# Program order for four operations of each float64 weight piece on ScalarE and VectorE

## The chip, the cores and the metric

The kernel runs on one core of a Trainium2 chip. The metric is the device time of one execution in microseconds (us). A core has five instruction streams: TensorE (PE in the profile, with its weight loads as PEld), VectorE (DVE), ScalarE (ACT), GpSimd (POOL) and SyncE (SP), which here only issues transfers. In the trace each engine takes its instructions in the order in which they stand in its stream; one that waits holds up those behind it.

## The reference

```python
X = np.fft.rfft(x, axis=1)                       # x: 8 x 3072 x 256, float32
Xr, Xi = (X.real.astype(np.float32), X.imag.astype(np.float32))
Yr = Xr @ w_r - Xi @ w_i + b_r                   # w_r, w_i: 256 x 256
Yi = Xr @ w_i + Xi @ w_r + b_i
Yr = np.sign(Yr) * np.maximum(np.abs(Yr) - lam, 0.0)      # lam = 0.01; Yi likewise
y = np.fft.irfft(Y, n=x.shape[1], axis=1).astype(np.float32)
...
h = x @ w_in                                     # 24576 rows; w_in 256 x 2048, w_out 2048 x 256: float64
g = np.where(h > 0.0, h, alpha * (np.exp(np.minimum(h, 0.0)) - 1.0))
x = (g @ w_out).astype(np.float32)
...
expert_idx = np.argmax(x @ w_gate, axis=1)       # 8 experts, each takes the first 768 rows that choose it
h = np.maximum(np.einsum('ecd,edf->ecf', disp, w1), 0.0)  # w1: 8 x 256 x 1024, w2: 8 x 1024 x 256
y = np.einsum('ecf,efd->ecd', h, w2)
out[i] = gate_w[i] * y[expert_idx[i], pos[i]]    # rows over the capacity stay zero
```

The inputs w_in and w_out of the middle layer are float64; the kernel has to turn them into float32 pairs itself.

## The kernel before

The kernel has three stages that overlap. In the first, three of the eight batches go through a Fourier transform, a mixing matrix and the transform back; as soon as some of it is there, the middle layer (`Moe.up`, `Moe.down`) begins on tiles of 512 rows; at the end the eight experts run. By then every expert has its 768 rows, so the other batches are never computed.

The first stage is cut into units. One batch has 12 units of work, numbered u0 to u35 over the three batches. The steps, with the lines that the profile shows:

- `s1` (L143 on PE, copies `zo` L145 on ACT, stores to `zs`): the first transform step, 8 pieces in a batch, from tiles `xp` that SP loads.
- `s2` of a unit (L173 on PE): needs the tile `zi`, which SP loads two units ahead into one of three buffers, and for the first 12 units a constant tile `ag`. Its result is split on ACT (`xr` L185, `im` L186, `xs` L199), DVE (`sm` L197, `xr` L198) and POOL (L200).
- `mix` of a unit (L218, L223, L229 on PE; in the plan 2.2 units after its `s2`), then `k` L220 on ACT, `tt` L233 on DVE, `kb` L235 on ACT, `tc` L236 on DVE.
- `i1` (L248 on PE), once for two units, reads their `tc`; ACT copies the result to two tiles `vo` (L252) and stores them to `vs`.
- `i2` (L272 on PE), 16 pieces in a batch, reads tiles `vi` that SP loads from `vs`; ACT copies it into the one buffer `yt` (L273), and every second time stores that to `ys`, from which the middle layer loads its rows `y`.

PSUM banks are shared: `s1`, `i1` and `i2` take turns on three banks (`pd`), `mix` on three others. So a late `zo`, `vo` or `yt` copy on ACT holds up the third PE step behind it.

Into this stage the float64 weights are worked, in 16 pieces of 128 x 512 values, called p0 to p15 here (8 of w_in, 8 of w_out). `f64_parts` handles one piece in four steps, which the plan puts at 0, 1.35, 1.5 and 1.85 units from the piece's time; pieces follow each other every 27/16 units. SP loads the raw words into the tile `fv` (512 KB); ACT squares the high words (L388); DVE selects (L390), shifts the low words out of `fv` (L392), and builds the float32 value (L393, L394); ACT rounds it to the first part (L396); DVE (L397, L399) and POOL (L398, L400) make the second part. The pool of these tiles has one buffer, so `fv` of a piece can be loaded only after L392 of the piece before, its last reader.

What order do the engines see? The Python code is traced in the plan's order. A scheduler then sorts each engine's stream: an instruction whose inputs it takes as ready goes ahead of one that would still wait, and of two ready ones the one that was traced first goes first. All loads on SP are exempt, since `load` wraps them:

```python
def load(tc, dst, src, eng=None):
    tc.keep_in_program_order((eng or tc.nc.sync).dma_start(dst, src))
```

`keep_in_program_order` ties an instruction behind the one that was traced just before it on the same engine. It adds no wait; it only fixes the place in the stream.

Of the kernel before, what the change touches and what calls it, by code (L numbers as in the profile page):

```python
# [14 lines left out]
AF = mybir.ActivationFunctionType  # L15
ALU = mybir.AluOpType
# [94 lines left out]
def load(tc, dst, src, eng=None):  # L111

    tc.keep_in_program_order((eng or tc.nc.sync).dma_start(dst, src))


def f32(ap):
    return ap.bitcast(F32)
# [256 lines left out]
def f64_parts(tc, tmp, src, p1, p2):  # L374

    nc, n = tc.nc, int(np.prod(src.shape[1:]))
    v = tmp.tile([128, 2 * n], I32, name="fv").rearrange("p (n t) -> p n t", t=2)
    sv = src.bitcast(I32)
    load(tc, v, sv.rearrange("p (n t) -> p n t", t=2) if len(sv.shape) == 2
                      else sv.rearrange("p a (n t) -> p a n t", t=2))  # L380
    yield
    hi, lo = v[:, :, 1], v[:, :, 0]
    sq = tmp.tile([128, n], F32, name="fsq")
    h = tmp.tile([128, n], I32, name="fh")
    a = tmp.tile([128, n], I32, name="fa")
    b = tmp.tile([128, n], I32, name="fb")
    least = float(np.array([0x380C0000], np.uint32).view(np.float32)[0])
    nc.scalar.activation(sq, f32(hi), AF.Square)  # L388
    yield
    nc.vector.scalar_tensor_tensor(f32(h), sq, least * least, f32(hi), op0=ALU.is_ge, op1=ALU.mult)  # L390
    low = sq.bitcast(I32)
    nc.vector.tensor_scalar(low, lo, 1, None, op0=ALU.logical_shift_right)  # L392
    nc.vector.tensor_scalar(a, h, 3, 0x3FFFFFF8, op0=ALU.logical_shift_left, op1=ALU.bitwise_and)  # L393
    nc.vector.scalar_tensor_tensor(b, h, -0x40000000, a, op0=ALU.bitwise_and, op1=ALU.bitwise_or)  # L394
    yield
    nc.scalar.copy(p1, f32(b))  # L396
    nc.vector.tensor_scalar(a, b, -0x00800000, None, op0=ALU.bitwise_and)  # L397
    nc.gpsimd.tensor_tensor(f32(b), f32(b), f32(p1), op=ALU.subtract)  # L398
    nc.vector.scalar_tensor_tensor(f32(h), low, 2.0 ** -51, f32(a), op0=ALU.mult, op1=ALU.mult)  # L399
    nc.gpsimd.tensor_tensor(p2, f32(b), f32(h), op=ALU.add)  # L400


# [9 lines left out]
def f64_piece(tc, tmp, w_in, w_out, win, wout, i):  # L412

    if i < 8:
        a, c = divmod(i, 4)
        sl = slice(c * 512, c * 512 + 512)
        return f64_parts(tc, tmp, w_in[a * 128:a * 128 + 128, sl], *(w[:, a, sl] for w in win))
    else:
        fs = slice(2 * (i - 8), 2 * (i - 8) + 2)
        return f64_parts(tc, tmp, w_out.rearrange("(f p) d -> p f d", p=128)[:, fs, :],  # L420
                  *(w[i - 8].rearrange("p f d -> p (f d)") for w in wout))
# [683 lines left out]
```

## Time and profile before

| what | value |
|---|---|
| median of 3 runs | 1209.8 us (1209.31 to 1209.97) |
| the profiled execution | 1211.05 us, of which its span (first to last instruction) is 1209.1 us |
| PE busy | 1164.1 us (96%) |
| DVE, ACT, POOL busy | 783.3 (65%), 721.6 (60%), 305.3 (25%) |
| mean granted TensorE clock | 0.985 of full speed |

The profiled execution lies 1.25 us above the median of the runs, and 1.95 us of it lie outside the span. PE is nearly always busy, so the time can only move where PE waits, or where its clock is lowered.

### The profile page before, as it was taken

Reading aid. Unit: us, or ns where it says so; the run is one execution under the profiler, and the core shown is the slowest. Engines: PE = TensorE matmul, PEld = TensorE weight load, DVE = VectorE, ACT = ScalarE, POOL = GpSimd, SP = SyncE. Lnnn points to the kernel's source line nnn. Section 1 sums busy time; section 2 is a strip of 40 time slices with the busy share of each in tenths; the row PEclk is TensorE's granted clock in tenths of the full one; section 3 lists DMA queues with packets and bytes.
Section 4 is the critical chain, followed back from the end, with each engine's and each line's share of the span. In section 5 each row is a group of like instructions: output and inputs, shape, how many; then the busy total and the mean of one; then the engine's idle time right before and its main releaser. Section 6 shows DMA issues by size and latency. Waiting matters only on the chain.

```text
span 1209.1 us, 21128 instructions
## 1 busy us (share of the span) xinstructions
PE 1164.1 (96%) x7800; PEld 1058.9 (88%) x7800; DVE 783.3 (65%) x2022; ACT 721.6 (60%) x1397; POOL 305.3 (25%) x347
## 2 busy tenths in 40 slices
PE   7799998999999999999999999999999999999994
PEld 2577797889999999999999999999999999999994
DVE  1588557553778777687777987887888544444430
ACT  4467676666776766656667666666665444444431
POOL 1244333310112222123122322222154211111111
PEclk9899898999999999999999999999999999999997
DMA  9888785644211211334225232222221323233300
GB/s 268 284 267 240 216 242 170 221 144 156 77 50 45 72 36 53 94 105 141 86 74 162 88 106 88 88 84 78 77 90 44 126 101 118 98 108 103 104 23 24
DMA packets 122912, 143.65 MB, mean 119 GB/s; under 512 B 9090, under 2 KB 106227, under 8 KB 122672
## 3 DMA queue, kind: packets, MB, share of 16 engines
q1 hardware_dynamic: 69360, 70.41, 19.5%
q10 hardware_dynamic: 48496, 59.17, 14.5%
q0 software_dynamic: 4944, 12.64, 3.0%
q8 instruction: 63, 1.03, 0.4%
q14 instruction: 49, 0.40, 0.1%
HBM read 71.96 MB, written 71.15 MB: 118 GB/s over the span
## 4 chain that ended last, share of the span: by engine, by line
PE 61%; issue 20%; DMA 6%; POOL 5%; DVE 4%; ACT 2%; POOLq 0%; SPq 0%; ACTq 0%; DVEq 0%
PE pm L486 25%; PE pa L463 24%; POOL out L405 4%; PE fi L272 3%; PE fmix L229 2%; PE fs L143 2%; PE fi L248 2%; PE fs L173 1%; DMA fv<-in_moe_w_in 1%; PE fmix L218 1%; DMA ys<-yt 1%; DMA zs<-zo 1%; DVE lw L515 1%; POOL g L471 1%; DMA xp<-in_x 1%
## 5 line engine op out<-in xcount | busy, mean ns | idle before, releaser
L486 PEld LDWEIGHTS pm<-wout,g 128*128 128x128 f32 x2640 | 346.1, 191 | 18.1 <-POOL g L471 1.3
L486 PE MATMUL pm<-wout,g 128*128 128x256 f32 x2640 | 352.7, 283 | 0.7 <-POOL g L471 0.5
L463 PE MATMUL pa<-x,win 128*128 128x512 f32 (+1 forms) x1344 | 345.4, 392 | 0.2 <-DVE e L469 0.2
L463 PEld LDWEIGHTS pa<-x,win 128*128 128x128 f32 x1344 | 236.9, 189 | 37.6 <-DVE e L469 0.7
L515 DVE SCALAR_TENSOR_TENSOR lw<-row,wg 128x256 bf16<-128x256 f32 x432 | 220.5, 510 | 7.0
L470 ACT CAST g<-e 128x512 fp32r<-128x512 f32 (+1 forms) x224 | 136.8, 612 | 127.9 <-DVE e L469 124.6
L469 DVE SCALAR_TENSOR_TENSOR e<-pa,e 128x512 f32<-128x512 f32 (+1 forms) x224 | 151.0, 678 | 77.5 <-ACT e L468 77.2
L467 ACT ACTIVATE e<-pa 128x512 f32<-128x512 f32 (+1 forms) x224 | 132.0, 590 | 70.0 <-PE pa L463 63.1
L471 DVE TENSOR_TENSOR g<-e,g 128x512 fp32r<-128x512 f32 x170 | 123.3, 727 | 66.3 <-ACT g L470 63.4
L668 DVE SCALAR_TENSOR_TENSOR eh<-eup,eh 128x384 fp32r<-128x384 f32 x128 | 71.1, 557 | 137.6 <-ACT eh L667 137.5
L666 PE MATMUL eup<-ex,ew 128*128 128x384 f32 x768 | 149.4, 340 | 0.3 <-DVE eh L668 0.3
L678 PE MATMUL edown<-ew,eh 128*128 128x256 f32 x1152 | 142.9, 280 | 0.0
L468 ACT ACTIVATE e<-e 128x512 f32<-128x512 f32 (+1 forms) x224 | 139.2, 625 | 5.2 <-ACT e L467 0.6
L678 PEld LDWEIGHTS edown<-ew,eh 128*128 128x128 f32 x1152 | 139.3, 188 | 0.0
L471 POOL TENSOR_TENSOR g<-e,g 128x512 fp32r<-128x512 f32 (+1 forms) x54 | 66.7, 1239 | 274.5 <-ACT g L470 207.6
L666 PEld LDWEIGHTS eup<-ex,ew 128*128 128x128 f32 x768 | 130.8, 188 | 0.8 <-DVE eh L668 0.6
L405 POOL DMA_INDIRECT out<-eo,er x48 | 46.7, 973 | 213.2 <-ACT eo L681 212.9
L667 ACT ACTIVATE eh<-eup 128x384 fp32r<-128x384 f32 x128 | 62.9, 492 | 60.4 <-PE eup L666 60.2
L681 ACT ACTIVATE eo<-edown,er 128x256 f32<-128x256 f32 x48 | 22.8, 475 | 89.8 <-PE edown L678 46.2
L405 POOL DMA_INDIRECT tab<-row,sl x55 | 57.2, 1040 | 51.7 <-DVE sl L570 38.6
L143 PE MATMUL fs<-xp,f 96*96 96x512 f32 x96 | 50.8, 665 | 10.0 <-DMA xp<-in_x 5.4
L272 PE MATMUL fi<-f,vi 96*128 96x96 f32 (+1 forms) x384 | 49.4, 272 | 3.1 <-DMA vi<-vs 2.6
(125 smaller groups left out, 1211.1 us busy)
## 6 DMA issues: line engine op xcount, KB each, us to landing
out<-row ACTq DMA_DIRECT2D x48, 512.0 KB, 3.5
ewraw<-in_moe_w SPq DMA_DIRECT2D x29, 512.0 KB, 3.6
xp<-in_x SPq DMA_DIRECT2D x24, 384.0 KB, 5.6
zs<-zo ACTq DMA_DIRECT2D x24, 384.0 KB, 5.0
zi<-zs SPq DMA_DIRECT2D x36, 256.0 KB, 5.1
vs<-vo ACTq DMA_DIRECT2D x36, 256.0 KB, 2.8
vi<-vs SPq DMA_DIRECT2D x48, 192.0 KB, 2.7
y<-ys SPq DMA_DIRECT2D x26, 256.0 KB, 3.6
```

Of the source, the lines that this page charges most:

```text
L272: nc.tensor.matmul(pv[:, j, :], v[:, j, :], self.k["f2"][:, 0:m])
L405: i = tc.nc.gpsimd.indirect_dma_start(dst, bass.IndirectOffsetOnAxis(idx, 0), src, None, bounds_check=rows - 1, oob_is_err=False)
L463: nc.tensor.matmul(ps, l, r, start=n == 0, stop=n == len(ops) - 1)
L467: nc.scalar.activation(e, ps, AF.Exp)
L468: nc.scalar.activation(e, e, AF.Relu, bias=1.0, scale=-1.0)
L469: nc.vector.scalar_tensor_tensor(e, ps, 0.0, e, op0=ALU.max, op1=ALU.subtract)
L470: nc.scalar.copy(g1, e)
L471: (nc.gpsimd if (f % 4 == 3 or self.tiles[c] < 4) and f < NF - 1 else nc.vector).tensor_tensor(g2, e, f32(g1), op=ALU.subtract)
L486: nc.tensor.matmul(self.pm[c][h][:, o, :], l[:, ts], r[f // 2][:, f % 2, :], start=f == 0 and o == 0 and n == 0, stop=f == NF - 1 and (o = ...
L515: self.tc.keep_in_program_order(v.scalar_tensor_tensor(T("lw", [128, D], BF16), row[:, t, 0:D], 1.0, rt["wg"][:, e, :], op0=ALU.mult, op1= ...
L666: nc.tensor.matmul(ps, l, r, start=i == 0, stop=i == len(ops) - 1)
L678: nc.tensor.matmul(ps, l[:, f, ts], r[:, f, :], start=f == 0 and i == 0, stop=f == NFE - 1 and i == 2)
```

## The change

Four of the operations of each piece are wrapped in `keep_in_program_order`: both on ACT, and on DVE the two that read what ACT or another step made. The instructions, their operands, buffers and loads stay the same. One line is added to the file, so that the line numbers from 388 on are one higher in the changed kernel (L389 is its square, L391 its select, L393 its shift).

```diff
     least = float(np.array([0x380C0000], np.uint32).view(np.float32)[0])
-    nc.scalar.activation(sq, f32(hi), AF.Square)
+    inorder = tc.keep_in_program_order
+    inorder(nc.scalar.activation(sq, f32(hi), AF.Square))
     yield
-    nc.vector.scalar_tensor_tensor(f32(h), sq, least * least, f32(hi), op0=ALU.is_ge, op1=ALU.mult)
+    inorder(nc.vector.scalar_tensor_tensor(f32(h), sq, least * least, f32(hi), op0=ALU.is_ge, op1=ALU.mult))
     low = sq.bitcast(I32)
     nc.vector.tensor_scalar(low, lo, 1, None, op0=ALU.logical_shift_right)
     nc.vector.tensor_scalar(a, h, 3, 0x3FFFFFF8, op0=ALU.logical_shift_left, op1=ALU.bitwise_and)
     nc.vector.scalar_tensor_tensor(b, h, -0x40000000, a, op0=ALU.bitwise_and, op1=ALU.bitwise_or)
     yield
-    nc.scalar.copy(p1, f32(b))
+    inorder(nc.scalar.copy(p1, f32(b)))
     nc.vector.tensor_scalar(a, b, -0x00800000, None, op0=ALU.bitwise_and)
     nc.gpsimd.tensor_tensor(f32(b), f32(b), f32(p1), op=ALU.subtract)
-    nc.vector.scalar_tensor_tensor(f32(h), low, 2.0 ** -51, f32(a), op0=ALU.mult, op1=ALU.mult)
+    inorder(nc.vector.scalar_tensor_tensor(f32(h), low, 2.0 ** -51, f32(a), op0=ALU.mult, op1=ALU.mult))
     nc.gpsimd.tensor_tensor(p2, f32(b), f32(h), op=ALU.add)
```

How the streams of the engines change: SP's stays as it was, row by row. On ACT and DVE the operations of every piece move to a later place among the others (by 3 to 19 rows on ACT, by 0 to 11 on DVE), up to the end of p15. PE's stream changes only in the first and the second batch, up to the mix of u17, and the same instructions stand in it.

DVE at the first piece (p0), before. `fs_391`, `fs_473` and `fs_523` are the `s2` results of u2, u3 and u4; `k_415` and `k_497` belong to the mix of u0 and u1:

```order
L198 TENSOR_TENSOR xr_364<-fs_358,xr_363 128x512
L192 MEMSET xe 128x4
L390 SCALAR_TENSOR_TENSOR fh<-fsq,fv 128x512
L392 TENSOR_SCALAR fsq<-fv 128x512
L393 TENSOR_SCALAR fa<-fh 128x512
L394 SCALAR_TENSOR_TENSOR fb<-fh,fa 128x512
L197 TENSOR_TENSOR sm<-fs_391,im 128x256
L198 TENSOR_TENSOR xr_397<-fs_391,xr_396 128x512
```

The same place in DVE's stream in the changed kernel:

```order
L197 TENSOR_TENSOR sm<-fs_391,im 128x256
L198 TENSOR_TENSOR xr_397<-fs_391,xr_396 128x512
L197 TENSOR_TENSOR sm<-fs_473,im 128x256
L233 TENSOR_TENSOR tt<-fmix,k_415 128x512
L198 TENSOR_TENSOR xr_479<-fs_473,xr_478 128x512
L236 SCALAR_TENSOR_TENSOR tc<-tt,kb 128x512
L391 SCALAR_TENSOR_TENSOR fh<-fsq,fv 128x512
L233 TENSOR_TENSOR tt<-fmix,k_497 128x512
L393 TENSOR_SCALAR fsq<-fv 128x512
L394 TENSOR_SCALAR fa<-fh 128x512
```

The shift that frees `fv` (L392, now L393) has moved behind the `tc` of u0 and the `tt` of u1.

ACT at the fourth piece (p3), as a piece of the difference. `fi_758` is the first half of the second `i1`, `fs_741` the `s2` of u7:

```order
 L199 CAST xs_691<-sm 128x256
-L185 CAST xr_746<-fs_741 128x512
 L186 COPY im<-fs_741 128x256
-L388 ACTIVATE fsq<-fv 128x512
-L235 ACTIVATE kb<-tt,lam 128x512
+L252 COPY vo<-fi_758 128x512
+L235 ACTIVATE kb<-tt,lam 128x512
+L397 CAST win_79<-fb 128x512
 L199 CAST xs_748<-sm 128x256
-L252 COPY vo<-fi_758 128x512
+L253 DMA vs_73<-vo 128x2x256
```

The square of p3 stood ahead of the copy `vo`; now it stands 13 rows behind that copy (the cast L397 here is that of p2).

PE at the first `i2` (`fi_1482`), before. `fs_1490` is the `s2` of u17, `fi_1507` and `fi_1508` are the `i1` of u14 and u15:

```order
L272 MATMUL fi_1482<-f_141,vi 128x96 x4
L173 MATMUL fs_1490<-ag_471,zi 128x2x64 x4
L248 MATMUL fi_1507<-tc,ag_302 128x256
L248 MATMUL fi_1508<-tc,ag_302 128x256
L248 MATMUL fi_1507<-tc,ag_302 128x256
```

The same in the changed kernel, where `fs_1584` is the `s2` of u18 and `xs_1415` belongs to the mix of u16; the `s2` of u17 and the whole mix of u15 stand ahead of these rows:

```order
L173 MATMUL fs_1584<-ag_521,zi 128x2x64 x4
L218 MATMUL fmix<-wr_147,xs_1415 128x256
L272 MATMUL fi_1482<-f_141,vi 128x96 x4
L248 MATMUL fi_1507<-tc,ag_302 128x256
L248 MATMUL fi_1508<-tc,ag_302 128x256
```

Two `s2`, one mix and the first matmul of another have moved ahead of the first `i2`.

## Rows read from the trace of the kernel before

**Rows 1.** Busy time by stage: engines' busy us (instructions), clock, DMA share, GB/s

```profile
40.00:130.00 90.00, 84.19 (x559) 66.81 (x557) 74.55 (x129) 61.57 (x134) 41.27 (x38) 0.98 0.82 255
130.00:245.00 115.00, 106.96 (x781) 94.73 (x782) 69.05 (x118) 74.48 (x151) 39.28 (x38) 0.94 0.69 209
245.00:860.00 615.00, 614.85 (x4036) 560.12 (x4036) 460.71 (x1340) 409.28 (x726) 138.76 (x163) 1.00 0.28 91
```

**Rows 2.** Waits of PE from 40 us on: us in total, times, longest

```profile
PE fi L248 <- ACT yt L273: 4.3, 1, 4.3
PE fmix L223 <- ACT k L220: 2.8, 3, 1.4
PE fi L272 <- DMA vi<-vs: 2.6, 1, 2.6
PE fs L143 <- ACT vo L252: 2.3, 1, 2.3
```

**Rows 3.** Waits of SP's queue, 40 to 230 us, same columns

```profile
SPq L113 <- DVE fsq L392: 35.2, 9, 7.5
```

**Rows 4.** Timeline of SP at p1: start us, us, issue

```profile
50.82 0.33 SPq L113 DMA_DIRECT2D fv<-in_moe_w_in  x1
...
51.67 0.43 SPq L113 DMA_DIRECT2D zi<-zs  x1
52.14 0.47 SPq L113 DMA_DIRECT2D ag<-in_cst  x1
```

**Rows 5.** Tile fv: ns min/median/max, first to last start, and its loads' landing

```profile
L388 ACT ACTIVATE fsq<-fv x16: 660/682/693, 48.2 to 204.9; 128x512 f32<-128x512 f32 x16
L390 DVE SCALAR_TENSOR_TENSOR fh<-fsq,fv x16: 678/692/1214, 49.6 to 205.6; 128x512 f32<-128x512 f32 x16
L392 DVE TENSOR_SCALAR fsq<-fv x16: 414/428/950, 50.3 to 206.4; 128x512 int32<-128x512 int32 x16
...
DMA to landing us min/median/max: 3.7/6.4/7.4
```

**Rows 6.** Landing of the loads of tile zi (36 loads), then of ag (12)

```profile
DMA to landing us min/median/max: 3.0/5.1/7.6
...
DMA to landing us min/median/max: 5.1/5.7/6.5
```

**Rows 7.** Timeline of ACT: the kb of u0

```profile
55.15 0.74 ACT L235 ACTIVATE kb<-tt,lam 128x512 f32<-128x512 f32 x1
```

**Rows 8.** Timeline of PE: s2 of u5, i1, mix of u3, s1

```profile
59.05 1.05 PE L173 MATMUL fs<-ag,zi 128*128 128x128 f32 x8
60.04 2.00 PE L248 MATMUL fi<-tc,ag 64*128 64x256 f32 x16
61.97 0.97 PE L218 MATMUL fmix<-wr,xs 128*128 128x256 f32 x6
...
64.44 2.04 PE L143 MATMUL fs<-xp,f 96*96 96x512 f32 x4
```

**Rows 9.** Timeline of ACT: the square of p3 [idle before, releaser]

```profile
76.26 0.66 ACT L388 ACTIVATE fsq<-fv 128x512 f32<-128x512 f32 x1 [2.00 <-DMA fv<-in_moe_w_in]
```

**Rows 10.** Timelines of PE and SP: the first i2, fv of p9, the first vi

```profile
131.84 2.00 PE L272 MATMUL fi<-f,vi 96*128 96x96 f32 x8 [2.59 <-DMA vi<-vs]
...
120.98 0.37 SPq L113 DMA_DIRECT2D fv<-in_moe_w_out  x1
129.00 1.39 SPq L113 DMA_DIRECT2D vi<-vs  x3
```

**Rows 11.** Busy time in two stretches, columns as in rows 1

```profile
75.00:80.00 5.00, 2.69 (x13) 1.33 (x12) 3.33 (x6) 2.91 (x6) 1.76 (x2) 1.00 0.75 214
131.80:140.30 8.50, 8.46 (x36) 6.62 (x37) 4.33 (x7) 4.33 (x8) 4.29 (x4) 0.60 0.92 257
```

**Rows 12.** Timelines of SP and PE: the last load into fv, and a wait of PE

```profile
214.82 0.49 SPq L113 DMA_DIRECT2D fv<-in_cst  x1
...
232.53 0.50 PE L223 MATMUL fmix<-bias,row 128*128 128x512 f32 x1 [1.20 <-ACT k L220]
```

## The prediction, made before the changed kernel had run

> **What bounds the kernel now.** I read the page first: PE is busy for 96% of the span, and the windows by stage show where the rest is [rows 1]. From 245 to 860 us PE works for 614.85 of 615 us, behind everything that this change moves. Whatever the stage of 40 to 245 us gains or loses therefore shifts the end by as much. In that stage PE idles 5.8 us up to 130 us and 8.0 us from there to 245 us, and its clock is granted at 0.98 and 0.94. The waits of PE [rows 2] name the idle time: 4.3 us once for `yt`, 2.8 us in three waits for `k`, 2.6 us once for `vi`, 2.3 us once for `vo`.
>
> Next I looked at SP, the queue that feeds all of this in a fixed order. It waits 35.2 us for the shift L392, nine times, up to 7.5 us [rows 3]. The reader should see that the shift is what frees `fv`: until it has run, the next load of `fv` cannot be issued, and the loads behind it stand still too. The timeline of SP at p1 shows who they are [rows 4]: after `fv` at 50.82 us come a `zi` at 51.67 and an `ag` at 52.14, both for the `s2` of u5. So the change acts on the time through one chain: later square, select or shift, later `fv`, later `zi` (and later `vi`), later PE. The tile view [rows 5, 6] gives its links.
>
> **The change part by part.** No operation is added or removed, so no engine's busy time changes. I work out six shifts.
>
> *The first piece.* In the changed order the shift of p0 stands behind the `tc` of u0, the select and the `tt` of u1. That `tc` needs the `kb` of u0, which ends at 55.15 + 0.74 = 55.89 us [rows 7]. Four operations of DVE follow: three that I price like the select of the same shape, 0.69 us, and the shift with 0.43 [rows 5], together 2.5. That gives 58.4, and with 0.2 for the release 58.6 us for `fv` of p1, 7.8 later than now. Keeping the distances within SP's queue, `zi` goes at 59.45 and `ag` at 59.9; with the median landings of 5.1 and 5.7 [rows 6] they are there at 64.55 and 65.6. In the changed order PE has an `i1` and most of a mix ahead of this `s2`: 59.05 + 1.93 + 2.47 = 63.45 us [rows 8]. That `i1` reads the `tc` of u1, now late too; by the queue of DVE that is about 0.9 us. PE then waits from 64.4 to 65.6, 1.2 us. Together 2.1, taken as **+2.0**; the bounds are 0 (`zi` and `ag` land at their minima, 3.0 and 5.1, and the mix covers more) and 4.5 (their maxima, 7.6 and 6.5).
>
> *The seven pieces up to 130 us (p2 to p8).* A piece cannot go round faster than landing, square, select and shift: 6.4 + 0.68 + 0.69 + 0.43 = 8.2 us [rows 5], with queueing 8.3 to 8.4. The pieces come at (204.9 − 48.2)/15 = 10.4 us. So the lag of some 8 us can be worked off only in part, and as the four operations now stand behind others each time, I let it stay at 8 to 10 us. The `zi` loads behind each `fv` then come just in time, and each piece costs between nothing and what a late landing adds, 7.6 − 5.1 = 2.5 us. I take 2.5 for the tightest place, the `s2` of u10 behind `fv` of p4, and a mean of 0.37 for the six others, as only a landing well over the median shows there: **+4.7**. The bounds are 0 and 7 × 2.5 = 17.5.
>
> Here a rule bears on the trace. The load of `fv` takes 6.4 us at the median, 3.7 at least [rows 5]. The Trainium skill, "DMA: Bandwidth & Descriptors", section "Anatomy of one DMA — SWDGE (gpsimd) path", fits a transfer by itself as 2.0 us plus its bytes over 436 thousand per us; for 512 KB that gives an estimate of 3.2 us, for transfers that GpSimd issues. The trace differs: half of these loads take twice that. By the page's figure each round would be 3.2 us shorter, the lag would be gone after two pieces, this term near 0.5 and the sum near −5.4.
>
> *Credits on ACT.* The 2.3 us wait for `vo` comes from the square of p3: it stands ahead of that copy and waits 2.00 us for its `fv` [rows 9]. In the changed order the square stands 13 rows behind the copy, so this wait goes. One of the `k` waits, the longest with 1.4 us, has the same cause. **−3.7**; bounds 0 and −5.1 (all of rows 2's `k` and `vo`).
>
> *The gap at the first `i2`.* PE waits 2.59 us for `vi` [rows 10], and in the 8.5 us behind it the clock is granted at 0.60 [rows 11], which costs 8.5 × (1 − 0.60) = 3.4 us of PE's work; together 6.0. In the changed order two `s2` (0.99 each) and a mix (2.47) [rows 8] move ahead of this `i2`, 4.4 us of work. Is `vi` later by more? It stands behind the `fv` of p9 on SP, now at 120.98, and goes at 129.00 [rows 10]. With a lag of 9.5 to 12 us that `fv` goes at 130.5 to 133, `vi` 0.5 later, and with the 2.84 us from issue to PE's start it is usable at 133.8 to 136.3. PE comes to the `i2` at 131.84 − 2.59 + 3.0 (the terms above) + 4.4 = 136.65. So the gap closes, and the lower clock behind it too: **−6.0**; bounds 0 and −6.0. Nothing of that 4.4 us is lost, as the work is only done earlier.
>
> *A new wait behind it.* The `i1` behind that `i2` reads the `tc` of u15, and the mix of u15 now stands closer ahead. `k`, `tt`, `kb`, `tc` are some 2.9 us at 0.7 each [rows 5, 7]; an `s2` and half an `i2` cover 2.0 of them: **+1.0**, bounds 0 and 2.9.
>
> *What stays.* The `yt` wait of 4.3 us [rows 2] hangs on the store of the `yt` before it, which moves with PE; I give it +0.3. At the end of the stage one load into the same tile goes at 214.82 and PE waits 1.20 us for a `k` at 232.53 [rows 12]; the shift of p15 comes some 1.3 us later against PE, of which about 0.5 shows: **+0.8** together, bounds 0 and 2.5.
>
> The sum: 2.0 + 4.7 − 3.7 − 6.0 + 1.0 + 0.8 = **−1.2 us**. The profiled execution took 1211.05 us (a span of 1209.1 and 1.95 around it), so I expect 1209.85 of a profile like it; the median of the runs, 1209.8, lies 1.25 below that execution, and I forecast 1208.6 us for it.
>
> **The rivals.** *A: slower through one new wait.* If the `zi` for the `s2` of u10 lands at its maximum and the queue is late too, PE waits there about 4.4 us in place of the 2.5 above. What decides is the length at which the clock goes down. After the 2.3 us wait for `vo` the stretch was granted 1.00, after the 2.59 us wait for `vi` 0.60 [rows 11]. Beyond some 2.5 us a second stretch like that would cost 3.4 us more: 1.9 + 3.4 = 5.3 on top of the sum, 1213.9 us. For it speaks that SP's order is fixed, so nothing overtakes a late `fv`; against it that such a wait needs a landing far above the median.
>
> *B: faster, as the late loads are hidden.* The lag may be worked off sooner, or PE may have enough other work before each `s2`. Then the seven pieces cost 1.0 in place of 4.7, while the two credits stay: −4.9, 1204.9 us. For it speak the shortest landings (3.7 for `fv`, 3.0 for `zi`), and that `zi` is loaded two units ahead. The rule of the skill's page above would lead to this case as well. Against it: nine waits of SP's queue on the shift already now, before anything is later.
>
> *C: slower, as the first `i2` waits again.* If the `fv` of p9 lags by more than 12.5 us, `vi` is late in spite of the 4.4 us of work ahead, the wait of 2.6 us is back and the clock with it: 6.0 more than the sum, 1214.6 us. The margin that I worked out is only 0.3 to 2.9 us.
>
> That nothing moves at all is excluded by the order of the streams; that all of it cancels is my forecast.
>
> **How the numbers follow.** The sum 0.40, A 0.13, B 0.35, C 0.12. The runs lie within 0.05% of each other; 0.2% (2.4 us) is about what a measurement can tell from no change. The sum's own range is 1206.2 to 1211.0, nearly all of it within 0.2%; B lies nearly wholly on the faster side, A and C on the slower. So: faster 0.36, same 0.39, slower 0.25. The two largest unknowns are the seven pieces and the gap at `i2`. A range from 1203.9, where the pieces cost nothing, to 1214.6, the time of C, leaves about one in ten on each side.
>
> **What the profile after would show.** The first shift near 58 us and `fv` of p1 at 58.6; a PE wait for `zi` or `ag` near 65 us. No wait for `vo` near 78 us. No wait for `vi` at the first `i2`, a clock near 1.00 behind it, and the `vi` load at 131 to 133.5. Waits for `zi` at some of the `s2` between 70 and 130 us, 4.7 us in all. The prediction is wrong if SP's wait for the shift doesn't move the `zi` loads, if PE's waits for `zi` sum up to under 2 or over 10 us by 130 us, or if a stretch of low clock appears at a place of its own.

## The result, and the profile after

The changed kernel is slower: 1224.1 us median of 4 runs (1221.52 to 1226.72) against 1209.9 us (1209.31 to 1212.32), a ratio of 1.0114 with an interval of 1.0088 to 1.0139. In later runs it was 1224.9 against 1211.6 us, a ratio of 1.0095 (1.0066 to 1.0124). The forecast was 1208.6 us, with a range from 1203.9 to 1214.6.

The profiled execution took 1221.52 us, of which the span is 1219.7. Its busy time by stage, columns as in [rows 1]:

```profile
40.00:130.00 90.00, 82.06 (x521) 64.16 (x520) 66.10 (x117) 55.93 (x123) 34.30 (x34) 0.95 0.74 225
130.00:245.00 115.00, 105.82 (x758) 92.61 (x758) 71.15 (x123) 74.16 (x151) 44.19 (x42) 0.96 0.72 219
245.00:860.00 615.00, 614.85 (x4048) 560.20 (x4045) 457.03 (x1321) 408.91 (x729) 139.14 (x165) 1.00 0.29 93
```

From 245 to 860 us PE is as full as before, so nearly all of the loss lies ahead of that stretch (what is lost behind it is told below). Up to 130 us PE ran 38 instructions fewer than in [rows 1] and at 0.95 instead of 0.98; and the DMA engines did less (0.74 instead of 0.82), although the same loads were due. The waits of PE from 40 us on (us in total, times, longest):

```profile
PE fi L272 <- DMA vi<-vs: 5.3, 2, 2.7
PE fs L173 <- DMA ag<-in_cst: 4.5, 2, 3.3
PE fmix L223 <- ACT k L220: 2.6, 1, 2.6
PE fs L143 <- ACT vo L252: 1.5, 1, 1.5
```

New against [rows 2] are 4.5 us for `ag`, and the `vi` wait stands there twice instead of once; the `yt` wait of 4.3 us is no longer among the large ones. SP's wait for the shift, to be held against [rows 3], with what stands behind it at p1 (the timeline of SP, against [rows 4]):

```profile
SPq L113 <- DVE fsq L393: 105.9, 16, 12.2
```

```profile
58.31 0.33 SPq L113 DMA_DIRECT2D fv<-in_moe_w_in  x1
...
59.27 0.62 SPq L113 DMA_DIRECT2D zi<-zs  x1
59.94 0.51 SPq L113 DMA_DIRECT2D ag<-in_cst  x1
```

The wait has tripled, from 35.2 to 105.9 us, and all three loads are 7.5 to 7.8 us later. In all SP does not wait longer: summed over the rows of that view, from 40 to 230 us, it is 146.8 us before and 147.7 after. Before, more of it was for buffers that PE had not yet read (43.1 us for `i2`, 25.7 for `s2`; now 3.7 and 9.3). So the queue stood more often at a load that came ahead of its need, and now stands at `fv`, with needed loads behind it. What PE makes of that (its timeline, then the chain of work that ended last at the same place, then the windows with the columns of [rows 1]):

```profile
67.50 2.05 PE L173 MATMUL fs<-ag,zi 128*128 128x128 f32 x8 [3.30 <-DMA ag<-in_cst]
...
69.78 3.62 PE L143 MATMUL fs<-xp,f 96*96 96x512 f32 x4
```

```profile
59.94 7.43 DMA ag<-in_cst
```

```profile
67.00:70.00 3.00, 2.50 (x11) 2.53 (x12) 1.81 (x4) 1.03 (x2) 1.52 (x1) 0.50 1.03 309
70.00:73.00 3.00, 3.00 (x4) 0.96 (x4) 1.62 (x3) 1.61 (x5) 1.62 (x3) 0.50 1.08 371
```

`ag` took 7.43 us to land, PE waited 3.30 us, and behind the wait the granted clock is 0.50, which is the lower level of 1.2 GHz, for 6 us: the eight matmuls of `s2` took 2.05 us (1.05 in [rows 8]), the four of `s1` 3.62 (2.04). That is some 3 us more.

**Where the time goes, unit by unit.** L223 stands once in each mix, in the same order in every version, so the start of the n-th L223 marks the n-th unit. Counted from the mark of u0 (46.62 us before, 46.49 after), the u4 mark is at 67.92 before and 74.93 after: 7.1 us behind. The same for the two profiles of the changed kernel and for those of e1 to e5, in us behind the kernel before:

| kernel | u4 | u6 | u10 | u14 | u17 | u29 | u33 |
|---|---|---|---|---|---|---|---|
| changed | 7.1 | 5.3 | 4.4 | 6.9 | 6.1 | 6.4 | 8.4 |
| changed, second profile (e11) | 7.3 | 5.5 | 7.3 | 8.2 | 11.0 | 11.6 | 17.2 |
| only p0 in program order (e1) | 7.7 | 6.0 | 7.1 | 9.4 | 8.6 | 7.7 | 8.9 |
| all but p0 (e2) | −0.1 | −2.3 | −2.3 | 0.0 | 0.5 | 0.1 | 1.6 |
| cast and multiplication only (e3) | 0.4 | 3.5 | 5.7 | 9.9 | 10.7 | 5.3 | 11.0 |
| changed, two `fv` (e4) | 0.2 | 2.8 | 0.8 | 2.8 | 4.1 | 2.8 | 8.4 |
| changed, load of p1 later (e5) | 0.2 | 5.3 | 4.5 | 6.5 | 5.5 | 4.1 | 8.0 |

Most of the loss of the first profile is there at u4. A profile is one execution: the two of the changed kernel differ by 0.2 us at u4 and u6, but by 2.9 at u10 and by 8.8 at u33, and e8 below, whose order is that of the changed kernel up to p9, is 5.1 behind at u4 after a wait of 2.59 us there. So a difference of some us between two marks behind u6 says little by itself. Behind u33 the span grows from 8.4 to 10.6 us more than before; 1.7 of these 2.2 us are lost near 933 us, in the experts' part, to the clock (last section).

### The profile page after: what moved, and what is told of

It is laid out like the page before. It is cut to its first block, busy times and chain, and to the rows that moved or that the text cites. A ratio compares the mean times of both kernels' runs of the same rounds, so it can differ in the third digit from the quotient of the medians.

```text
span 1219.7 us, 21134 instructions
## 1 busy us (share of the span) xinstructions
PE 1170.7 (96%) x7800; PEld 1063.2 (87%) x7800; DVE 781.2 (64%) x2022; ACT 719.7 (59%) x1397; POOL 305.1 (25%) x347
## 4 chain that ended last, share of the span: by engine, by line
PE 63%; issue 19%; DMA 6%; POOL 5%; DVE 3%; ACT 2%; SPq 0%; POOLq 0%; ACTq 0%; DVEq 0%
PE pm L487 24%; PE pa L464 24%; POOL out L406 4%; PE fi L272 3%; PE fs L143 2%; PE fmix L229 2%; DMA ys<-yt 2%; PE fi L248 2%; PE fs L173 2%; DMA ag<-in_cst 2%; PE fmix L218 1%; PE eup L667 1%; DMA vi<-vs 1%; POOL g L472 1%; DVE lw L516 1%
## 5 line engine op out<-in xcount | busy, mean ns | idle before, releaser
L668 ACT ACTIVATE eh<-eup 128x384 fp32r<-128x384 f32 x128 | 62.7, 492 | 60.8 <-PE eup L667 59.9
L272 PEld LDWEIGHTS fi<-f,vi 96*128 96x128 f32 x384 | 47.0, 192 | 9.2 <-issue 4.6
```

What stands on the lines that cost most here:

```text
L272: nc.tensor.matmul(pv[:, j, :], v[:, j, :], self.k["f2"][:, 0:m])
```

## The experiments

Beside e1 to e12 single runs of the kernel before lay between 1205.0 and 1215.6 us; its median was 1210.7 to 1212.2 in the four groups. So the runs spread over 0.9%, where the prediction had taken 0.05% from three of them. Differences of medians under about 2.5 us say nothing there.

**e1 and e2: the first piece, and the others.** `f64_parts` gets a parameter; e1 sets `keep=i == 0`, e2 `keep=i > 0`:

```diff
-    inorder = tc.keep_in_program_order
+    inorder = tc.keep_in_program_order if keep else (lambda i: i)
```

Expected of e1: 

> Only the four operations of the first piece (p0) keep program order; p1 to p15 are as before. Theory L (one late load): the loss is made once, at the s2 of u5, where the late first shift makes fv of p1, and with it zi and ag, late by some 7.5 us, so that PE waits 3.3 us and then runs at a low clock. It expects most of the loss back: a wait for ag of about 3 us near 67 us and 1216 to 1221 us. Rival M (many late loads): each piece costs a little, the first no more than the others; it expects under 1213 us.

Expected of e2: 

> The four operations of p1 to p15 keep program order, those of p0 don't. Theory L expects no wait for ag at u5 and a time within 5 us of the kernel before (1207 to 1215 us). Rival M expects 1218 to 1224 us, nearly all of the loss. If both this kernel and the one with only p0 lose less than the whole, the two add up.

Measured: e1 1220.7 us, 9.9 above the kernel before (ratio 1.0074, 1.0052 to 1.0096). e2 1215.4 us, 4.6 above (1.0039, 1.0018 to 1.0061). The two add up to 14.5 us, and the whole change costs 14.2; each of the two is known to some 2.6 us. The timeline of PE in e1, then in e2:

```profile
67.24 2.05 PE L173 MATMUL fs<-ag,zi 128*128 128x128 f32 x8 [4.26 <-DMA ag<-in_cst]
```

```profile
86.83 1.13 PE L173 MATMUL fs<-ag,zi 128*128 128x128 f32 x8 [2.15 <-DMA ag<-in_cst]
```

In e1 the wait at u5 is there, in e2 it isn't; e2 has one at u10, and nothing near 78 us, where the kernel before waits 2.3 us for `vo`. So about two thirds come from the first piece, and about a third from the others: theory L holds for most of the loss, M for the rest.

**e3: only the last two operations.** The square and the select lose their wrappers, the cast and the multiplication keep them:

```diff
-    inorder(nc.scalar.activation(sq, f32(hi), AF.Square))
+    nc.scalar.activation(sq, f32(hi), AF.Square)
...
-    inorder(nc.vector.scalar_tensor_tensor(f32(h), sq, least * least, f32(hi), op0=ALU.is_ge, op1=ALU.mult))
+    nc.vector.scalar_tensor_tensor(f32(h), sq, least * least, f32(hi), op0=ALU.is_ge, op1=ALU.mult)
```

Expected: 

> The square and the select are free again; only the last two (the cast to the first part on ScalarE and the multiplication on VectorE) keep program order. The place of the shift in VectorE's stream is that of before for p0 (row 26) and at most 4 rows later for the others. Both theories put the loss on the shift and so expect 1208 to 1214 us. A rival by which the late last steps cost the time (the cast and the multiplication hold up copies of the transform) expects 1217 us or more.

Measured: 1219.8 us, 9.0 above the kernel before (1.0066, 1.0039 to 1.0093). Both theories missed this; the rival was right in its time. The timeline of PE, then of ACT, and the window behind PE's first wait (columns of [rows 1]):

```profile
79.13 1.84 PE L143 MATMUL fs<-xp,f 96*96 96x512 f32 x2 [3.68 <-ACT vo L252]
...
244.50 2.08 PE L248 MATMUL fi<-tc,ag 64*128 64x256 f32 x8 [4.52 <-DVE tc L236]
```

```profile
75.75 0.66 ACT L389 ACTIVATE fsq<-fv 128x512 f32<-128x512 f32 x1 [3.38 <-DMA fv<-in_moe_w_in]
```

```profile
79.00:82.00 3.00, 2.87 (x8) 1.81 (x9) 0.06 (x1) 0.94 (x3) 2.90 (x3) 0.56 0.49 175
```

There is no wait at u5. But the wait for `vo` near 78 us, which was 2.3 us long before, is now 3.68: the square of p3 still stands ahead of that copy and waits 3.38 us for its `fv`, and the cast of p2 stands ahead of it too. Behind it the clock is at 0.56. So the kernel before has a second place at which a little more lateness costs several us (3.5 at u6), and it is enough to move the last two operations to reach it.

**e4: a second buffer for `fv`, in the changed kernel.** `fv` moves to a pool of its own:

```diff
-        fp["f64"] = mk(f64st, "f64", 1)
+        fp["f64"] = {"t": mk(f64st, "f64", 1), "fv": mk(f64st, "f64v", 2)}
```

Expected: 

> The changed kernel with two buffers for fv (a pool of its own), so that the load of a piece waits for the shift two pieces back; the order of the four operations on ScalarE and VectorE stays within 5 rows of the changed kernel. Theory L and M (the shift acts only through SyncE's queue) expect the wait at u5 to be gone and 1203 to 1212 us. The rival that the later places of the operations on ScalarE and VectorE cost the time by themselves expects 1218 us or more.

Measured: 1216.6 us, 5.8 above the kernel before (1.0056, 1.0035 to 1.0078), between both expectations. SP's wait for the shift fell to 24.3 us, and the wait at u5 is gone. What is left begins at the `vo` copy (timelines of PE, then ACT, then DVE):

```profile
79.10 1.10 PE L143 MATMUL fs<-xp,f 96*96 96x512 f32 x2 [3.60 <-ACT vo L252]
```

```profile
75.89 0.40 ACT L199 CAST xs<-sm 128x256 fp32r<-128x256 f32 x1 [2.90 <-DVE sm L197]
...
78.47 1.06 ACT L252 COPY vo<-fi 128x512 f32<-128x512 f32 x2
```

```profile
72.07 0.69 DVE L392 SCALAR_TENSOR_TENSOR fh<-fsq,fv 128x512 f32<-128x512 f32 x1 [1.19 <-POOL win L402]
...
75.38 0.42 DVE L197 TENSOR_TENSOR sm<-fs,im 128x256 f32<-128x256 f32 x1
```

Read from below: the select waits for GpSimd's addition of the piece before (it reads `fh`, which has one buffer); behind the select all of the piece's work on DVE runs before `sm`; ACT's `xs` waits for `sm`, and `vo` stands behind `xs`. So by the medians (14.2 us fall to 5.8) the late loads are the larger part of the loss, and the places of the operations cost too, here through the `vo` copy.

Not all that e3 and e4 lose lies on these paths. By the marks 5.7 us of e3 and 5.6 of e4 fall between u29 and u33, where an `i1` waits for a `tc` (4.52 us in e3, above; 4.49 in e4). The chain of work leads from there over `kb` to ACT's cast of the rows `y`, which stands ahead of it, and to the load of these rows. That load in the kernel before, then in e3:

```profile
229.98 3.54 DMA y<-ys
```

```profile
235.19 6.71 DMA y<-ys
```

It took 6.69 us in e4; in e5 6.26, with a wait of 4.08 us at this `i1`, and in e11 5.23, with 3.04. Neither theory names this load, and why it takes longer is not shown.

**e5: p1's load behind three others.** In the changed kernel:

```diff
-            at(t + d, t + d, [w_load if d == W_STAGES[0] else lambda i=i: next(parts[i], None)])
+            d2 = d + 0.35 * (i == 1 and d == W_STAGES[0])
+            at(t + d2, t + d2, [w_load if d == W_STAGES[0] else lambda i=i: next(parts[i], None)])
```

Expected: 

> The changed kernel; only the load of fv for p1 is planned 0.35 units later, which puts it behind three loads in SyncE's queue (xp, and zi and ag of u5). Nothing else of the four operations' order is undone. If the 10 us that the first piece costs come from the loads that stand behind this fv in the queue, the 3.3 us wait at u5 and the low clock behind it go, and the time falls by 5 to 10 us from the changed kernel's, to 1214 to 1219 us. If they come from the later places of the first square, select and shift as such, it stays at 1221 to 1226 us.

Measured: 1220.6 us (1.0092, 1.0063 to 1.0122): between the two expectations, and not to be told from the changed kernel. But the mechanism shows plainly. The timelines of PE and SP:

```profile
75.01 2.05 PE L173 MATMUL fs<-ag,zi 128*128 128x128 f32 x8 [4.82 <-DMA ag<-in_cst]
```

```profile
67.40 0.33 SPq L113 DMA_DIRECT2D fv<-in_moe_w_in  x1
67.83 1.19 SPq L113 DMA_DIRECT2D zi<-zs  x1
69.06 0.47 SPq L113 DMA_DIRECT2D ag<-in_cst  x1
```

At u5 PE no longer waits; u4 is only 0.2 us behind. The wait has moved to the next load that stands behind an `fv`, that of p2, and the `ag` of u7: 4.8 us. So the queue is the cause at u5, and the lag, if not worked off, is handed on.

**e6 and e7: controls on the kernel before.** e6 has e4's second buffer; e7 plans every load of `fv` later:

```diff
-W_STAGES = 0, 1.35, 1.5, 1.85
+W_STAGES = 0.35, 1.35, 1.5, 1.85
```

Expected of e6: 

> The kernel before with two buffers for fv: the control for the changed kernel with two buffers. If waiting for fv is what its squares hold the vo copy for, the 2.3 us wait near 78 us goes and the time is 2 to 6 us below the kernel before (1204 to 1209 us). If the earlier loads of fv only compete with those of zi and ag, it is 1 to 6 us above.

Expected of e7: 

> The kernel before, with every load of fv planned 0.35 units later (W_STAGES starts at 0.35), so that at some pieces a zi stands ahead of fv in SyncE's queue. Where the zi loads bind, it is faster by 1 to 5 us; where the late fv binds (the square waits for it and holds the vo copy), slower by 2 to 8 us. I expect the second, near 1214 us, as the 2.3 us wait for vo lies at the point where the clock begins to fall.

Measured: e6 1211.9 against 1210.7 us (1.0010, 0.9996 to 1.0025), e7 1208.4 (0.9992, 0.9974 to 1.0009): no difference for either, and my expectations were wrong, slower for e7 and faster for e6. In e6 the 2.3 us wait for `vo` is gone, as expected, but PE waits 2.1 us for a `k` and 1.7 for a `tc` elsewhere. So a second buffer gives nothing in the kernel before, and e4's gain belongs to the late queue of the changed one.

**e8: p9's load behind the first `vi`.** As e5, with `0.1 * (i == 9 ...)`.

Expected: 

> The changed kernel; the load of fv for p9 is planned 0.1 units later, so that the first two vi loads stand ahead of it in SyncE's queue; TensorE's order at the first i2 then is that of the kernel before again. Theory Q (the vi is held by the late fv p9 in the queue, as rival C of the prediction had it): vi goes several us earlier and PE's wait for it is under 1 us. Rival S (the vi waits for the store vs<-vo that it reads from, which landed at 138.7 us, 0.1 us ahead of the issue of vi): vi is issued no more than 2 us earlier, and as PE comes to the i2 earlier, it waits 4 us or more. The time then is 0 to 4 us above the changed kernel's.

Measured: 1225.4 us (1.0105, 1.0058 to 1.0152). The timelines of PE and SP, and the store on the chain of work:

```profile
140.42 1.99 PE L272 MATMUL fi<-f,vi 96*128 96x96 f32 x8 [6.38 <-DMA vi<-vs]
```

```profile
137.36 0.86 SPq L113 DMA_DIRECT2D vi<-vs  x2
138.31 0.43 SPq L113 DMA_DIRECT2D fv<-in_moe_w_out  x1
```

```profile
129.11 8.19 DMA vs<-vo
```

The store began at 129.11 and landed at 137.3, and `vi` went 0.06 us later, with no `fv` ahead of it. PE, which comes there earlier, waits 6.4 us. Rival S holds: it is the store that `vi` waits for, not the `fv`. The next two runs show the same: in e9 and e10 the store took 8.13 and 8.19 us, and PE waited 6.28 and 6.42 us for `vi`.

**e9 and e10: later loads in the changed kernel, with and without p0.** e7's edit, on the changed kernel and on e2.

Expected of e9: 

> The changed kernel with every load of fv planned 0.35 units later: a few zi (at u5, p5 and p7) and vi loads then stand ahead of fv. If the late fv only hands its lag on to the next load in the queue, as the kernel with p1's load late showed, the time stays at 1218 to 1224 us; if the right order of the queue cures it, it is 1208 to 1214 us. I expect the first.

Expected of e10: 

> p0 free, p1 to p15 in program order, all loads of fv planned 0.35 units later. With p0 free 1215.4 us were measured, with the wait for ag at u10 of 2.2 us the largest before 130 us. The later loads put a zi ahead of two fv there. I expect 1210 to 1216 us; under 1209 us it would be a version at least as good as the kernel before.

Measured: e9 1221.1 us (1.0063, 1.0040 to 1.0087), e10 1215.4 us (1.0036, 1.0015 to 1.0058). Both are as expected: another order of SP's queue doesn't cure it, and e10 is where e2 was.

**e11: the changed kernel again.** Expected: 

> The changed kernel itself, on the chip of these runs: 1220 to 1227 us. If the 1.5 us wait near 933 us lowers the clock by chance, about half of such profiles show a granted clock near 0.7 behind it and half 1.00.

Measured: 1224.9 us (1.0095, 1.0066 to 1.0124). The waits at u5 (3.67) and at the first `i2` (3.25) repeat. At 938 us the clock was 1.00 (last section). Behind the first `i2` it was not; the window there (columns of [rows 1]):

```profile
143.00:150.00 7.00, 7.00 (x25) 4.26 (x25) 3.82 (x7) 3.23 (x6) 0.72 (x1) 0.57 0.42 96
```

**e12: a try at a version faster than both.** e7's edit, and

```diff
-    uf = fp["f64"].tile([128, 1024], I32, name="fv").bitcast(F32)[:, 0:128]
+    uf = rtp.tile([128, 128], F32, name="uf")
```

Expected: 

> A try at a version faster than both: the kernel before with every load of fv planned 0.35 units later, and with the last small load that shared fv's tile (uf, from cst) in a tile of its own, so that it need not wait for the shift of p15, nor VectorE 2.5 us for it. The y loads and the casts that read them then move up by some rows. If the late small load is what PE waits 1.2 us for near 232 us, it is 1 to 3 us below the kernel before (1207 to 1210 us); if the casts that have moved up hold other copies on ScalarE, it is 2 to 8 us above.

Measured: 1211.7 against 1212.2 us (1.0004, 0.9987 to 1.0020), no difference. A 1.67 us wait for a `k` was still there. None of the twelve is measurably faster than the kernel before.

## Why the prediction was wrong

The chain that the prediction argued from (later shift, later `fv`, later `zi` and `ag`, later PE) is what happened, and e5 shows it. Two terms of the sum failed, the first piece by its size and the gap at the first `i2` by its mechanism; they account for 9.3 of the 9.6 us between the sum and the profile at u33. The upper end of the range, 6.0 above the sum, was the time of one rival alone, so the two misses together went beyond it. By the marks of the first profile, in us:

| term | forecast | measured | from |
|---|---|---|---|
| the first piece | +2.0 | +7.1 | mark of u4 |
| seven pieces, with the credits on ACT | +4.7 − 3.7 = +1.0 | −0.2 | u4 to u14 |
| the gap at the first `i2`, the wait behind it | −6.0 + 1.0 = −5.0 | −0.8 | u14 to u17 |
| what stays, and the end of the stage | +0.8 | +2.3 | u17 to u33 |
| sum | −1.2 | +8.4 | u33 |

*The first piece* was mis-sized, beyond its own upper bound of 4.5. The issue times came out as worked out: `fv` 58.31 (forecast 58.6), `zi` 59.27 (59.45), `ag` 59.94 (59.9), and the `tc` of u1 cost 0.37 us. PE came to the `s2` of u5 at 64.20 (64.4). (The 0.2 us for the release, which the prediction takes from no row, was 0.05: the shift ended at 58.26.) Two prices were wrong. I let `ag` land in 5.7 us, the median of its twelve loads. Seven loads go out together here, in both kernels, and the very load that I was pricing, the one issued at 52.14, had taken 6.5 us, the longest of all. The view of that tile over that one load says so:

```profile
L113 SPq DMA_DIRECT2D ag<-in_cst x1: 465/465/465, 52.1 to 52.1; - x1
DMA to landing us min/median/max: 6.5/6.5/6.5
```

After, it took 7.43, nearly a microsecond more again. So PE waited 3.30 us in place of 1.2. And I priced the wait without the clock, which stood at 0.50 behind it: about 3 of the 7 us. These two, 2.1 and 3.0, are the 5.1 us by which the term missed. Rival A had exactly this pair, a wait and the lower clock behind it, but at u10, and with a chance of 0.13. (At u10 PE waits 1.21 us in the first profile; in e11 it waits 2.44, and the clock is granted at 0.64 from 95 to 99 us.) What SP's standing still did to the transfers is seen in the windows from 52 to 58 us, before and then after (columns as in [rows 1]):

```profile
52.00:58.00 6.00, 6.00 (x44) 5.14 (x43) 4.84 (x8) 3.98 (x10) 3.50 (x3) 1.00 0.92 307
```

```profile
52.00:58.00 6.00, 6.00 (x43) 5.23 (x42) 3.71 (x7) 4.92 (x14) 1.47 (x2) 1.00 0.00 0
```

A share of 0.92 became 0.00: for 6 us nothing was moved at all, and the same burst followed later, with less of PE's work left to cover it.

*The seven pieces and the credits* were about right as a sum, and not in their parts. The waits of 2.3 us for `vo` and 1.35 for `k` are gone, as forecast (−3.7); new ones for `ag` (1.21) and `vo` (1.50) and smaller ones put 3.5 on the other side, where 4.7 stood. But the 4.7 were to be waits for `zi`, and no wait of PE up to 130 us is put down to a `zi`: by the prediction's own sign (under 2 us) that part was wrong, and that the sum fits is partly luck. The `k` wait had another cause than the one given, too. No square waits for `fv` there; the chain of work goes from `k` over the two `vo` copies to `sm`, which stood on DVE behind the select, the shift and the building of p4 (84.44 to 86.68 us). The credit for `vo` is confirmed by e2, which keeps it without the loss: 2.3 us ahead at u6.

*The gap at the first `i2`* failed in its mechanism. I took `vi` to stand behind the `fv` of p9. Both in the kernel before and after, another transfer ends the wait of SP: the store `vs<-vo`, from which `vi` reads. SP's waits in the kernel before (columns of [rows 3]; the longest is this one), then the chain of work at that place, before and after:

```profile
SPq L113 <- DMA vs<-vo: 10.5, 3, 7.6
```

```profile
125.04 3.89 DMA vs<-vo
...
129.00 2.70 DMA vi<-vs
```

```profile
131.11 7.61 DMA vs<-vo
...
138.79 4.13 DMA vi<-vs
```

The store begins 6.1 us later, as PE itself is 6.9 us behind at u14, and takes 7.61 instead of 3.89 us, with the DMA engines at 0.98 from 131 to 139 us (0.59 from 125 to 129 before). `vi` is 9.8 us later and lands 1.4 us slower, and the 4.4 us of work that moved ahead of the `i2` is used up: PE comes to it at 140.33 us (forecast 136.65), can start at 142.97 (forecast 136.3 at the latest) and waits 2.64 us, as before. Rival C forecast that wait, by another cause. Its condition, a lag of more than 12.5 us, was met: the `fv` of p9 went at 137.33 us, 16.4 later than before. But behind that `fv` SP waited 1.0 us more for the store, and in e8, with no `fv` ahead, `vi` went only 1.4 us earlier. Why the store takes twice as long is not shown.

Of the 6.0 us only the 3.4 of the lower clock went: the window from 130 to 160 us is granted 1.00. No part of the change explains that, and in e11 it did not hold. And 2.4 of the 3.4 us are lost again between 155 and 160 us: by the chain of work there, the store `ys<-yt` takes 7.25 us, the copy `yt` waits 3.08 for it, and the `i1` ahead of the mix of u17 runs in two halves of 1.99 us, one behind the other, where both together took 2.00 before. The row that I needed for `vi` is the one above, in the view of SP's waits, which names the transfer; I read that view only for the shift.

*What stays, and the end of the stage*: the `yt` wait of 4.3 us did not stay. In its place PE waits 2.68 us for a `vi` at 194.5, with the clock at 0.57 from 196 to 204 us, as it was before behind the `yt` wait (189 to 197). The wait for `k` near 232 us grew from 1.20 to 2.64 us, and the 5 us from 240 were granted 0.66 (1.00 before). The direction was right, the size was not, and it varies: from u17 to u33 the first profile loses 2.3 us, e11 6.2.

What stays open: how much each of the later pieces costs (e2's 4.6 us is a difference of medians; its profile, the fastest of its runs, shows 1.6 at u33); why the stores and the `y` load land late; and all of e3, which loses as much as e1 by other waits, so that the shift is not the only way to this loss. The counterpart of e3, with only the square and the select in program order, was not tried.

## What to carry to other kernels

Where one queue feeds everything in a fixed order, ask of each load not only what it waits for, but who stands behind it, and take its landing from the same load in the trace, not from the median of its kind. Price a new wait on TensorE together with the clock behind it, and of every transfer that ends a wait, ask which event released its issue. In this kernel every version that moved these operations back was slower, by 3.8 to 14.2 us, and none that only changed the loads of the kernel before (e6, e7, e12) was measurably faster. So a sum of small gains and losses here needed a range that is wider on the slow side.

## What the hardware showed that I had not expected

The length of a wait alone does not tell whether the clock falls behind it. In the profiles of the kernel before, of the changed one and of e11 there is the same wait at the start of the experts' work (timelines of PE, in this order, then the windows of 6 us from 1 us ahead of it):

```profile
924.53 0.18 PE L557 MATMUL pk<-oh,u 128*128 128x32 bf16 x1 [1.48 <-DVE ex L649]
```

```profile
932.87 0.18 PE L558 MATMUL pk<-oh,u 128*128 128x32 bf16 x1 [1.50 <-DVE ex L650]
```

```profile
938.88 0.18 PE L558 MATMUL pk<-oh,u 128*128 128x32 bf16 x1 [1.48 <-DVE ex L650]
```

```profile
923.50:929.50 6.00, 4.97 (x36) 4.97 (x36) 5.88 (x28) 2.72 (x7) 0.16 (x2) 1.00 0.00 0
```

```profile
931.80:937.80 6.00, 4.93 (x26) 4.93 (x25) 4.42 (x20) 1.15 (x3) 0.10 (x1) 0.72 0.00 0
```

```profile
937.80:943.80 6.00, 4.92 (x36) 4.92 (x36) 5.90 (x28) 2.69 (x7) 0.13 (x2) 1.00 0.00 0
```

The same instructions wait 1.5 us, and the clock behind it was 1.00, 0.72 and 1.00: 26 matmuls in the window instead of 36. In the same way, at the first `i2`, 2.59 us before [rows 10] were followed by 0.60, 2.64 us after by 1.00, and 3.25 in e11 by 0.57. So the 2.5 us from which rival A let it decide is no bound. Where the clock does fall, it costs 6 × (1 − 0.72) = 1.7 us here and some 3 at u5, and it can do so at one run's wait and not at the next.
